# Opening of a spectral mixing and SoLU kernel: rows passed between partitions on chip instead of through DRAM, and one queue for the loads

## The chip, the cores and the metric

The kernel runs on one core of one Trainium2 chip. A core has five engines that run side by side: TensorE (matrix products; PE in the profile), VectorE (DVE), ScalarE (ACT), GpSimd (POOL) and SyncE (SP), and 16 DMA engines that carry out the transfers the others issue. The metric is the time of one execution on the device in microseconds; lower is better.

## The reference

The input x has 8 batch elements of 3136 rows and 256 channels. Each channel is filtered by a Fourier transform along the rows, a product with a complex filter, and the transform back. The result, 25088 tokens of 256, goes through a feed-forward block: a product with w_in to 1024, SoLU (h times its softmax), a layer norm with gain g, and a product with w_out back to 256.

```python
def _attn_ref(x, filt_r, filt_i):
    X = np.fft.rfft(x, axis=1)
    F = (filt_r + 1j * filt_i)[None, :, :]
    return np.fft.irfft(X * F, n=x.shape[1], axis=1).astype(np.float32)

def _moe_ref(x, w_in, w_out, g_ln):
    h = x @ w_in
    e = np.exp(h - np.max(h, axis=-1, keepdims=True))
    sm = e / (np.sum(e, axis=-1, keepdims=True) + 1e-09)
    solu = h * sm
    mu = np.mean(solu, axis=-1, keepdims=True)
    var = np.mean((solu - mu) ** 2, axis=-1, keepdims=True)
    ln = (solu - mu) / np.sqrt(var + 1e-06) * g_ln
    return (ln @ w_out).astype(np.float32)
```

The weights w_in and w_out are 64-bit floats in memory; the kernel makes 32-bit floats of them with integer operations.

## The kernel before

The transform of 3136 = 49 × 64 rows is done in two steps. The first step (`pa`) is a product along the 49, with results for 25 residues s in four parts a, and 32 columns n. They lie with (s, a) along 100 partitions and n along the row. The second step works in seven *units* of up to four residues, and wants (a, n), 128 of them, along the partitions. So the rows have to change partitions twice: from the first step to the units (`t2`), and from the units (`g`) to the step back (`t4`, `py`). For all batch elements but the first this lies beside the main loop. For the first, element 0, it is the *opening*: nothing of the main loop can start before it.

In the kernel before, rows change partitions by way of DRAM: `store_first` writes them to `d1`, `fetch` reads them as units; `store` writes to `d2`, `fetch_back` reads. Unit 0 alone is passed on chip, by 16 small transfers.

```python
    d1 = [dram.tile([NS, P, C], FP32, name=f"d1_{e}") for e in range(B)]
    d2 = [dram.tile([NS, P, C], FP32, name=f"d2_{e}") for e in range(B)]
# ... (helpers of the class Spectrum)
        def first(self, i, halves, ps, evac, out=None):

            n0, n = 2 * halves[0], 2 * len(halves)
            if out is None:
                out = self.pools["t1"].tile([NK, n, C], FP32, name=f"t1_{self.e}_{i}_{n0}", tag="t1")
            self.t1s[i, n0] = t1 = out
            for j, u in enumerate(halves):
                nc.tensor.matmul(out=ps[0:NK, j], lhsT=wf_t, rhs=self.xs[i][0:NR, 2 * u:2 * u + 2, :],
                                 start=True, stop=True)
            evac(out=t1.rearrange("p n c -> p (n c)"), in_=ps[0:NK].rearrange("p a b -> p (a b)"))


        def store_first(self, i, n0, store):
            t1 = self.t1s.pop((i, n0))
            store(d1[self.e].rearrange("s (a n) c -> (s a) n c", a=4)[
                :, NCH * i + n0:NCH * i + n0 + t1.shape[1], :], t1)
# ...

        def fetch(self, i, dma, out=None):
            self.t2s[i] = self.buffer(i, "t2", [P, 4, C]) if out is None else out
            rows, n = self.rows(i, d1[self.e])
            dma(out=self.t2s[i][:, 0:n, :], in_=rows)
# ...
        def multiply(self, i, part, add):

            residues, w = self.shape(i)
            rows = slice(0, NQ * residues)
            f = self.fs[i][rows, 0:w]

            out, term = (self.buffer(i, kind, [P, 2, C])[rows, 0:w, :]
                         for kind in (("pr", "pi")[part], "pt"))
            re, im = (ps[rows, 0:w, :] for ps in self.spectra[i])
            nc.vector.tensor_tensor(out=out, in0=re, in1=f[:, :, part, :], op=ALU.mult)
            nc.vector.tensor_tensor(out=term, in0=im, in1=f[:, :, 1 - part, :], op=ALU.mult)
            add(out=out, in0=out, in1=term, op=(ALU.subtract, ALU.add)[part])
            self.prods.setdefault(i, []).append(out)
            if part == 1:
                del self.fs[i], self.spectra[i]

        def inverse(self, i, pss):
            de, prods = self.des.pop(i), self.prods.pop(i)
            for r in range(2):
                for u in range(self.shape(i)[0]):
                    rows = slice(NQ * u, NQ * u + NQ)
                    self.product(i, pss[u][NQ * r:NQ * r + NQ], lambda v: de[rows, v, 1, r, :],
                                 prods[r][rows])
            self.gs[i] = self.buffer(i, "g", [P, 4, C])
            for u in range(self.shape(i)[0]):
                w = self.shape(i)[1]
                nc.scalar.copy(out=self.gs[i][:, u:2 * w:2, :], in_=pss[u][:, 0:w, :])

        def store(self, i, dma):
            rows, n = self.rows(i, d2[self.e])
            dma(out=rows, in_=self.gs.pop(i)[:, 0:n, :])
```

What `convert` ends with, after its VectorE operations:

```python
            if share:
                nc.scalar.mul(rest, lo, 2.0 ** -44)
                nc.gpsimd.tensor_tensor(out=rest, in0=rest, in1=power.bitcast(FP32), op=ALU.mult)
            else:
                stt(out=rest, in0=lo, scalar=2.0 ** -44, in1=power.bitcast(FP32), op0=ALU.mult,
                    op1=ALU.mult)
            nc.gpsimd.tensor_tensor(out=dst, in0=dst, in1=rest, op=ALU.add)
```

The opening in program order:

```python
        st.enter_context(tc.manual_schedule())
        nc.sync.dma_start(out=wf_t, in_=wf_dram)
        pieces = NH // NCH

        fetch_x(0, 0, NCH, 0, N1 - 1, nc.sync.dma_start)
        fetch_x(0, 0, NH, N1 - 1, 1, nc.sync.dma_start)
        for i in range(pieces):
            if i:
                fetch_x(0, NCH * i, NCH, 0, N1 - 1, nc.sync.dma_start)
            fetch_x(1, NCH * i, NCH, 0, N1, nc.gpsimd.dma_start)
            if i in (4, 7):
                begin(i // 7)
        load_tables(0, 4, nc.gpsimd.dma_start)
        load_tables(4, 4, nc.gpsimd.dma_start)
        for i in range(pieces):
            sp.xs[i] = rows_x[:, NCH * i:NCH * i + NCH]

            sp.first(i, (0, 1), ps_h.tile([P, 2, 512], FP32, name=f"pa_0_{i}", tag="h"),
                     nc.scalar.copy, sp.xs[i][0:NK])
            sp.store_first(i, 0, lambda out, in_: by_16((nc.scalar.dma_start, nc.sync.dma_start), out, in_))

        def idle(out):

            nc.tensor.matmul(out=out, lhsT=tables[0][0][:, 0, 0].rearrange("p u q -> p (u q)"),
                             rhs=filters[0][0][:, 0], start=True, stop=True)

        def idle_row(count, name):
            for j in range(count):
                idle(ps_h.tile([P, 2, C], FP32, name=f"{name}_{j}", tag="h"))

        idle_row(8, "idle")

        def convert(j):
            load_float64(weights[j][0], raws.pop(j), negate=j < 4, share=j < 4)

        for j in range(2):
            convert(j)

# ...
        def start(i):
            sp.fetch_filter(i)
            sp.fetch_de(i)
            sp.forward(i, halves(f"pb_0_{i}"))

        units = len(sp.units)

        sp.t2s[0] = t2_0 = pools["t2"].tile([P, 4, C], FP32, name="t2_0_0", tag="t2")
        for n in range(16):
            (nc.sync, nc.scalar)[n % 2].dma_start(
                out=t2_0[NH * (n % 4):NH * (n % 4) + NH, n // 4, :], in_=rows_x[n:n + 1])
        for i in range(1, units):
            sp.fetch(i, nc.sync.dma_start, spare_piece(i - 1))
            if i == 2:
                load_tables(8, NP - 8, nc.sync.dma_start)
        for i in range(2):
            start(i)
        for i in range(units):
            if i + 2 < units:
                start(i + 2)
            sp.multiply(i, 0, nc.vector.tensor_tensor)
            sp.multiply(i, 1, nc.gpsimd.tensor_tensor)
            pss = [ps_t.tile([P, 2, C], FP32, name=f"pc_0_{i}_{u}", tag="t") for u in range(2)]
            idle(pss[0])
            sp.inverse(i, pss)
            sp.store(i, nc.scalar.dma_start)
            if i == 0:
                nc.gpsimd.dma_start(out=wi_t, in_=wi_dram)
                nc.gpsimd.dma_start(out=wq_t, in_=wq_dram)
                nc.gpsimd.dma_start(out=g_sb, in_=moe_g_ln.rearrange("(k p) -> p k", p=P))
            elif i != 2:
                begin({1: 2, 3: 3, 4: 4, 5: 5, 6: 6}[i])
        idle_row(14, "idler")
        rows_t4 = pools["r"].tile([P, NH, C], FP32, name="t4_0", tag="r")
        for ch in range(pieces):
            t4s[0, ch] = rows_t4[0:NK, NCH * ch:NCH * ch + NCH]
        for ch in range(pieces):
            fetch_back(0, ch, None, by_16)
        fetch_second()
        for i0, n, rows in ((0, 4, P), (4, 4, P), (8, NP - 9, P), (NP - 1, 1, NQ)):
            f, at = filters[i0]
            nc.sync.dma_start(
                out=f_dram[i0:i0 + n].rearrange("i u q k c -> (u q) i (k c)")[0:rows],
                in_=f[0:rows, at:at + n].rearrange("p i k c -> p i (k c)"))
        convert(2)
        begin(7)
        convert(3)
        convert(4)
        weight_sums(w_in_sb)
        for j in (5, 6, 7):
            convert(j)
        for ch in range(pieces):
            for cb in range(KD):
                back(0, ch, cb, nc.scalar.copy)
```

`fetch_x` loads rows of x, half h = 0 forward and h = 1 backward. `begin(j)` loads a piece of weights as 64-bit words (512 KB), `convert(j)` takes it apart: eight to ten VectorE operations, one or two GpSimd operations and, with `share`, a ScalarE scaling. `load_tables` loads the transform tables `de` and the filters `f`. `idle` is a product whose result nobody uses; it keeps TensorE at work while it would wait. The order of instructions on each engine is that of the program.

## Time and profile before

| | |
|---|---|
| time, median of 3 runs | 1681.72 us (1679.47 to 1682.98) |
| span of the profiled execution | 1680.2 us |
| TensorE busy | 1597.7 us (95%) |
| VectorE, ScalarE, GpSimd busy | 75%, 56%, 67% |
| moved by DMA | 311.72 MB, mean 186 GB/s |
| first product of the first step | at 9.34 us |
| first product of a unit (pb) | at 45.28 us |
| first product of the step back (py) | at 90.93 us |
| first product of the main loop (m) | at 107.50 us |

The profile names an instruction by its engine, its line in the kernel and its tiles, as `py<-wi_t,t` for what is written and read. Behind each group stands how long its engine sat idle before it, and what ended that. The chain of waits goes back from the last instruction to what released it, and so on; the stretches on it set the time, whatever other engines are doing.

### The profile page before, as it was taken

To read this page: it belongs to the slowest core of one execution; us is meant where nothing else is said; L and a number is where in the kernel's file an instruction comes from. 1 tells how busy PE (TensorE), PEld (TensorE's weight loads), DVE (VectorE), ACT (ScalarE), POOL (GpSimd) and SP (SyncE) were. 2 spreads that over 40 slices of the span, in tenths; PEclk is the share of its full clock that TensorE was granted. 3 is DMA by queue.
4 is the path that set the end of the run, shared out by engine and by line. 5 is a ranking of instruction groups with operands and counts; after the bars stand their busy time and mean duration, and the time that the engine had idled before them with its cause. 6 is when DMAs were issued, how large, how long until landed. Compare 5 with 4: busy or idle time off the path is not lost.

```text
span 1680.2 us, 31072 instructions
## 1 busy us (share of the span) xinstructions
PE 1597.7 (95%) x10022; PEld 1094.7 (65%) x10022; DVE 1260.4 (75%) x2619; ACT 939.3 (56%) x1730; POOL 1120.8 (67%) x1268
## 2 busy tenths in 40 slices
PE   5798899999999999999999999999999999999996
PEld 1353356766766676667766676667776777777776
DVE  1676887788777877886878777887778767787773
ACT  2154455656655565566655656556565566655551
POOL 4444786577676766697577866687576766676674
PEclk8999999999999999999999999999999999999999
DMA  9886868786787668865786667766775444444443
GB/s 264 254 278 202 255 180 243 196 220 182 191 224 222 178 182 236 228 182 150 210 243 195 176 166 220 229 181 161 204 213 161 117 125 123 103 106 105 109 112 95
DMA packets 375957, 311.72 MB, mean 186 GB/s; under 512 B 61514, under 2 KB 341571, under 8 KB 375795
## 3 DMA queue, kind: packets, MB, share of 16 engines
q1 hardware_dynamic: 306260, 169.81, 38.5%
q0 software_dynamic: 32640, 101.65, 20.5%
q10 hardware_dynamic: 36896, 38.28, 8.2%
q8 instruction: 81, 1.33, 0.3%
q14 instruction: 80, 0.66, 0.1%
HBM read 124.83 MB, written 81.50 MB: 123 GB/s over the span
## 4 chain that ended last, share of the span: by engine, by line
PE 64%; DMA 17%; DVE 8%; POOL 3%; issue 3%; SPq 2%; ACT 1%; ACTq 0%; DVEq 0%; POOLq 0%
PE m L680 26%; PE o L792 25%; DMA solu_t<-turn 7%; PE py L353 5%; DMA x<-in_x_dram 2%; DMA t<-d 2%; PE pa L260 2%; PE pb L292 2%; PE pc L292 2%; SPq L750 2%; DVE h L728 2%; DVE turn L738 1%; DMA out_dram<-ot 1%; PE pa L217 1%; DVE diff L245 1%
## 5 line engine op out<-in xcount | busy, mean ns | idle before, releaser
L730 ACT ACTIVATE e<-h,nmu 128x1024 f32<-128x1024 f32 x196 | 225.3, 1149 | 360.3 <-DVE h L728 358.8
L792 PEld LDWEIGHTS o<-w_out_sb,solu_t 128*128 128x128 f32 x3136 | 380.3, 192 | 57.8 <-issue 40.7
L792 PE MATMUL o<-w_out_sb,solu_t 128*128 128x128 f32 x3136 | 400.5, 276 | 9.1 <-DVE rsum L723 6.3
L680 PE MATMUL m<-w_in_sb,s 128*128 128x512 f32 x784 | 401.8, 604 | 4.6 <-ACT h L690 2.5
L792 PEld LDWEIGHTS o<-w_out_sb,u 128*128 128x128 f32 x2352 | 305.2, 191 | 147.4 <-issue 113.8
L658 POOL TENSOR_TENSOR u<-solu_t 128x512 f32<-128x512 f32 x98 | 145.3, 1483 | 311.0 <-DMA solu_t<-turn 179.0
L680 PE MATMUL m<-w_in_sb,y 128*128 128x512 f32 x588 | 313.8, 617 | 15.9 <-DVE nmax L704 12.8
L792 PE MATMUL o<-w_out_sb,u 128*128 128x128 f32 x2352 | 312.3, 276 | 7.0 <-ACT ot L804 6.3
L728 DVE SCALAR_TENSOR_TENSOR h<-e,rsum,h 128x1024 f32<-128x1024 f32 x196 | 289.1, 1475 | 6.9
L811 DVE SCALAR_TENSOR_TENSOR ot<-o,rs_t,ot 128x128 f32<-128x128 f32 x294 | 102.5, 349 | 206.6 <-ACT ot L804 170.3
L690 ACT COPY h<-m 128x512 f32<-128x512 f32 x294 | 173.5, 590 | 130.8 <-PE m L680 116.2
L738 DVE STREAM_TRANSPOSE turn<-h 128x1024 f32<-128x1024 f32 x196 | 242.3, 1236 | 0.8
L712 ACT ACTIVATE e<-h,nmax 128x1024 f32<-128x1024 f32 x196 | 226.1, 1154 | 0.0
L658 POOL TENSOR_TENSOR u<-solu_t,u 128x512 f32<-128x512 f32 x98 | 142.7, 1456 | 87.2 <-PE o L792 83.3
L704 DVE CUSTOM_DVE_ANT_0 h<-m,h 128x512 f32<-128x512 f32 x196 | 133.2, 679 | 82.2 <-ACT h L690 59.3
L680 PEld LDWEIGHTS m<-w_in_sb,y 128*128 128x128 f32 x588 | 95.1, 192 | 124.5 <-DVE nmax L704 67.9
L356 ACT COPY y<-py 128x392 f32<-128x392 f32 x128 | 109.6, 856 | 105.4 <-PE py L353 103.8
L353 PEld LDWEIGHTS py<-wi_t,t 100*128 100x128 f32 x1024 | 132.3, 192 | 53.9 <-issue 40.4
L680 PEld LDWEIGHTS m<-w_in_sb,s 128*128 128x128 f32 x784 | 124.0, 191 | 65.9 <-issue 45.7
L658 POOL TENSOR_TENSOR solu_t<-solu_t,solu_t 128x512 f32<-128x512 f32 x98 | 150.8, 1538 | 7.7
L658 POOL TENSOR_TENSOR u<-u,solu_t 128x512 f32<-128x512 f32 x98 | 136.9, 1397 | 0.7
L353 PE MATMUL py<-wi_t,t 100*128 100x98 f32 x1024 | 131.6, 273 | 0.7 <-DMA t<-d 0.4
(108 smaller groups left out, 1978.3 us busy)
## 6 DMA issues: line engine op xcount, KB each, us to landing
solu_t<-turn SPq DMA_DIRECT2D x784, 128.0 KB
out_dram<-ot SPq DMA_DIRECT2D x196, 128.0 KB
t<-d POOLq DMA_DIRECT2D x56, 400.0 KB, 4.9
d<-x POOLq DMA_DIRECT2D x100, 200.0 KB, 5.3
f<-f_dram POOLq DMA_DIRECT2D x39, 512.0 KB, 6.9
d<-g POOLq DMA_DIRECT2D x39, 512.0 KB, 5.1
t<-d ACTq DMA_DIRECT2D x36, 512.0 KB
x<-in_x_dram SPq DMA_DIRECT2D x112, 98.0 KB
```

The costliest lines, as they stand in the source:

```text
L353: nc.tensor.matmul(out=psv[:, i:2 * NCH - i:2 * NCH - 1 - 2 * i, :], lhsT=t4s[e, ch][:, i, cb * P:cb * P + P], rhs=wi_t, start=True, stop= ...
L356: evac(out=y[:, cb, t0:t0 + S].rearrange("p (r m j) -> p m j r", m=N2 // NCH, j=NCH)[:, ch:last + 1 - ch:last - 2 * ch], in_=psv.rearrange ...
L658: nc.gpsimd.tensor_tensor(out=out, in0=in0, in1=in1, op=op)
L680: nc.tensor.matmul(out=ms[j, bank], lhsT=lhsT, rhs=w_in_sb[:, w, :], start=m in (1, 2, 7), stop=True, skip_group_check=True)
L690: nc.scalar.copy(out=h_half(k, i), in_=ms[j, 0])
L704: nc.vector.tensor_tensor_reduce(out=h_half(k, i), in0=ms[j, bank], in1=h_half(*kept), scale=1.0, scalar=sofar, op0=ALU.add, op1=ALU.min, ...
L712: nc.scalar.activation(out=e, in_=hs[k], func=AFT.Exp, bias=nmaxs.pop(k)[:, 1:2], scale=-1.0, accum_out=esum)
L728: nc.vector.scalar_tensor_tensor(out=solu, in0=e, scalar=rsum, in1=solu, op0=ALU.mult, op1=ALU.mult, accum_out=nmu)
L730: nc.scalar.activation(out=e, in_=solu, func=AFT.Square, bias=nmu, scale=-float(DFF), accum_out=variances[g][:, i:i + 1])
L738: nc.vector.transpose(out=turns[g][:, :, i, :], in_=solus.pop(k).rearrange("p (f j) -> p f j", j=32))
L792: nc.tensor.matmul(out=pos[p, bank], lhsT=lhs[:, f, :], rhs=w[:, f, :], start=f == 0 and m in (1, 2, 7), stop=True, skip_group_check=True)
L811: nc.vector.scalar_tensor_tensor(out=ot, in0=pos[p, bank], scalar=rs, in1=out_half(p, *kept)[0], op0=ALU.mult, op1=ALU.add)
```

## The change

The change keeps the rows on chip. After the first step, 25 transfers, one for each residue, move 4 partitions × 32 rows of 256 to 128 partitions × one row; seven units use them. After the units, 25 transfers do the opposite. All are issued by GpSimd. The stores to `d1` and `d2` of element 0 and the fetches from them go away. All loads from DRAM in the opening move to SyncE's queue, in the order in which they are needed; the 49 rows of a half are loaded as 48 and 1, and as 45 and 4. Loads of weights come earlier, three of the eight conversions rather than two stand ahead of the units, and the rows of useless products are shortened from 8 to 6 and from 14 to 7. It is for a shorter wait between the first step, the units and the step back.

```diff
--- before.py
+++ after.py
@@ -163,15 +163,6 @@
                     yield (slice(NQ * u + 32 * quarter, NQ * u + 32 * quarter + 32), k, held,
                            filter_rows(filt, quarter, u, i0, held))
 
-    def whole(dmas, out, in_):
-        dmas[0](out=out, in_=in_)
-
-    def by_16(dmas, out, in_):
-
-        n = 45 if out.shape[0] == N1 else out.shape[0] // 16 * 16
-        dmas[0](out=out[:n], in_=in_[:n])
-        dmas[1](out=out[n:], in_=in_[n:])
-
     class Spectrum:
 
 
@@ -335,14 +326,12 @@
 
     t4s = {}
 
-    def fetch_back(e, ch, rows_pool, split=None):
-
-        split = split or whole
-        if rows_pool is not None:
-            t4s[e, ch] = rows_pool.tile([P, NCH, C], FP32, name=f"t4_{e}_{ch}", tag="r")[0:NK]
-        split(
-            (nc.sync.dma_start if split is by_16 else nc.gpsimd.dma_start, nc.sync.dma_start), t4s[e, ch],
-            d2[e].rearrange("s (a n) c -> (s a) n c", a=4)[:, NCH * ch:NCH * ch + NCH, :])
+    def fetch_back(e, ch):
+
+        t4s[e, ch] = pools["r"].tile([P, NCH, C], FP32, name=f"t4_{e}_{ch}", tag="r")[0:NK]
+        nc.gpsimd.dma_start(
+            out=t4s[e, ch],
+            in_=d2[e].rearrange("s (a n) c -> (s a) n c", a=4)[:, NCH * ch:NCH * ch + NCH, :])
 
     def back(e, ch, cb, evac):
 
@@ -366,7 +355,7 @@
 
         def load_words(src, n):
             raw = wpool.tile([P, 512, 2], I32, name=f"raw_{n}", tag="raw")
-            nc.gpsimd.dma_start(
+            nc.sync.dma_start(
                 out=raw.rearrange("p (k d) w -> p k d w", d=src.shape[-2]) if len(src.shape) == 4 else raw,
                 in_=src)
             return raw
@@ -470,22 +459,29 @@
         nc.sync.dma_start(out=wf_t, in_=wf_dram)
         pieces = NH // NCH
 
-        fetch_x(0, 0, NCH, 0, N1 - 1, nc.sync.dma_start)
-        fetch_x(0, 0, NH, N1 - 1, 1, nc.sync.dma_start)
+
         for i in range(pieces):
-            if i:
-                fetch_x(0, NCH * i, NCH, 0, N1 - 1, nc.sync.dma_start)
-            fetch_x(1, NCH * i, NCH, 0, N1, nc.gpsimd.dma_start)
-            if i in (4, 7):
-                begin(i // 7)
-        load_tables(0, 4, nc.gpsimd.dma_start)
-        load_tables(4, 4, nc.gpsimd.dma_start)
+            for h in range(2):
+                rows = (N1 - 1, N1 - 4)[h]
+                fetch_x(h, NCH * i, NCH, 0, rows, nc.sync.dma_start)
+                if i == 0:
+                    fetch_x(h, 0, NH, rows, N1 - rows, nc.sync.dma_start)
+            if i == 4:
+                begin(0)
+        begin(1)
+        for j, (i0, n) in enumerate(((0, 4), (4, 4), (8, NP - 8))):
+            load_tables(i0, n, nc.sync.dma_start)
+            if j < 2:
+                begin(j + 2)
+        nc.sync.dma_start(out=wi_t, in_=wi_dram)
+        nc.sync.dma_start(out=wq_t, in_=wq_dram)
+        nc.sync.dma_start(out=g_sb, in_=moe_g_ln.rearrange("(k p) -> p k", p=P))
+        begin(4)
         for i in range(pieces):
             sp.xs[i] = rows_x[:, NCH * i:NCH * i + NCH]
 
             sp.first(i, (0, 1), ps_h.tile([P, 2, 512], FP32, name=f"pa_0_{i}", tag="h"),
                      nc.scalar.copy, sp.xs[i][0:NK])
-            sp.store_first(i, 0, lambda out, in_: by_16((nc.scalar.dma_start, nc.sync.dma_start), out, in_))
 
         def idle(out):
 
@@ -496,13 +492,10 @@
             for j in range(count):
                 idle(ps_h.tile([P, 2, C], FP32, name=f"{name}_{j}", tag="h"))
 
-        idle_row(8, "idle")
+        idle_row(6, "idle")
 
         def convert(j):
-            load_float64(weights[j][0], raws.pop(j), negate=j < 4, share=j < 4)
-
-        for j in range(2):
-            convert(j)
+            load_float64(weights[j][0], raws.pop(j), negate=j < 4, share=j < 3)
 
         def start(i):
             sp.fetch_filter(i)
@@ -511,14 +504,32 @@
 
         units = len(sp.units)
 
-        sp.t2s[0] = t2_0 = pools["t2"].tile([P, 4, C], FP32, name="t2_0_0", tag="t2")
-        for n in range(16):
-            (nc.sync, nc.scalar)[n % 2].dma_start(
-                out=t2_0[NH * (n % 4):NH * (n % 4) + NH, n // 4, :], in_=rows_x[n:n + 1])
+
+        sp.t2s[0] = pools["t2"].tile([P, 4, C], FP32, name="t2_0_0", tag="t2")
         for i in range(1, units):
-            sp.fetch(i, nc.sync.dma_start, spare_piece(i - 1))
-            if i == 2:
-                load_tables(8, NP - 8, nc.sync.dma_start)
+            sp.t2s[i] = spare_piece(i - 1)
+
+        def residues(i):
+            for s in range(4 * i, min(4 * i + 4, NS)):
+                yield slice(4 * s, 4 * s + 4), s - 4 * i
+
+        convert(0)
+        for i in range(units):
+            for rows, s in residues(i):
+                nc.gpsimd.dma_start(out=sp.t2s[i][:, s, :], in_=rows_x[rows])
+            if i in (1, 3):
+                convert((i + 1) // 2)
+        for j in (5, 6, 7):
+            begin(j)
+        rows_t4 = pools["r"].tile([P, NH, C], FP32, name="t4_0", tag="r")
+        for ch in range(pieces):
+            t4s[0, ch] = rows_t4[0:NK, NCH * ch:NCH * ch + NCH]
+
+        def store(i):
+            g = sp.gs.pop(i)
+            for rows, s in residues(i):
+                nc.gpsimd.dma_start(out=rows_t4[rows], in_=g[:, s, :])
+
         for i in range(2):
             start(i)
         for i in range(units):
@@ -526,34 +537,22 @@
                 start(i + 2)
             sp.multiply(i, 0, nc.vector.tensor_tensor)
             sp.multiply(i, 1, nc.gpsimd.tensor_tensor)
+            if i:
+                store(i - 1)
             pss = [ps_t.tile([P, 2, C], FP32, name=f"pc_0_{i}_{u}", tag="t") for u in range(2)]
             idle(pss[0])
             sp.inverse(i, pss)
-            sp.store(i, nc.scalar.dma_start)
-            if i == 0:
-                nc.gpsimd.dma_start(out=wi_t, in_=wi_dram)
-                nc.gpsimd.dma_start(out=wq_t, in_=wq_dram)
-                nc.gpsimd.dma_start(out=g_sb, in_=moe_g_ln.rearrange("(k p) -> p k", p=P))
-            elif i != 2:
-                begin({1: 2, 3: 3, 4: 4, 5: 5, 6: 6}[i])
-        idle_row(14, "idler")
-        rows_t4 = pools["r"].tile([P, NH, C], FP32, name="t4_0", tag="r")
-        for ch in range(pieces):
-            t4s[0, ch] = rows_t4[0:NK, NCH * ch:NCH * ch + NCH]
-        for ch in range(pieces):
-            fetch_back(0, ch, None, by_16)
+        store(units - 1)
+        idle_row(7, "idler")
         fetch_second()
         for i0, n, rows in ((0, 4, P), (4, 4, P), (8, NP - 9, P), (NP - 1, 1, NQ)):
             f, at = filters[i0]
             nc.sync.dma_start(
                 out=f_dram[i0:i0 + n].rearrange("i u q k c -> (u q) i (k c)")[0:rows],
                 in_=f[0:rows, at:at + n].rearrange("p i k c -> p i (k c)"))
-        convert(2)
-        begin(7)
         convert(3)
-        convert(4)
         weight_sums(w_in_sb)
-        for j in (5, 6, 7):
+        for j in range(4, 8):
             convert(j)
         for ch in range(pieces):
             for cb in range(KD):
@@ -876,7 +875,7 @@
         assert S * (e - 1) <= P * (back_at[0] // 2 * 2) and P * (back_at[-1] + 2) <= S * e // P // 2 * 2 * P
         for ch, t in enumerate(back_at):
             row_loads.append((
-                t, t - 1, spectrum_at[-1] + 2, lambda e=e, ch=ch: fetch_back(e, ch, pools["r"])))
+                t, t - 1, spectrum_at[-1] + 2, lambda e=e, ch=ch: fetch_back(e, ch)))
             for cb in range(KD):
                 (early, late)[cb][t].append(
                     lambda e=e, ch=ch, cb=cb: back(e, ch, cb, nc.scalar.copy))
```

## The prediction

> **What bounds the kernel now.** I read the page first. Its first part gives TensorE 1597.7 us busy of a span of 1680.2 us, so the main loop is bound by matmuls and has nothing to give. The change touches only the opening, so the question is how long the opening is and which wait ends last in it. The second part shows where TensorE is not full:
>
> ```profile
> PE   5798899999999999999999999999999999999996
> ```
>
> Each digit is 42 us. Only the first four slices, 168 us, have room (the last is the tail, which is not changed). The largest gain that a perfect opening could bring is therefore some tens of microseconds, one or two per cent.
>
> Next I asked for the chain of waits over the first 110 us (start, length, what; the pieces of the units and those of a few hundredths are left out):
>
> ```profile
> 1.35 7.95 DMA x<-in_x_dram
> 9.34 8.51 PE pa L217 x12
> ...
> 18.92 7.71 DMA d<-x
> 26.70 6.53 DMA d<-x
> 33.25 8.10 DMA t<-x
> 41.37 4.71 DMA t<-x
> 46.09 7.40 DMA f<-in_filt_r_dram
> 53.51 5.59 DMA y<-d
> ...
> 78.88 12.21 PE idler L492 x28
> 91.09 0.88 PE py L353 x8
> ...
> 100.10 6.81 DMA y<-in_x_dram
> ...
> 108.21 5.83 DMA f_dram<-f
> ```
>
> From 18.92 to 59.10 us the chain is nothing but transfers: rows of the first step out to DRAM (d<-x), back in (t<-x, y<-d), and one table load (f) between them. The 12.21 us of "idler" are matmuls without a use; they fill the wait for the second round trip (d<-g, then t<-d). After 91 us come the first step back (py, 16.6 us long) and the main loop, whose first product starts at 107.50.
>
> Third, the windows of these stages (duration, busy time of TensorE, its weight loads, VectorE, ScalarE, GpSimd, granted clock, DMA share, GB/s):
>
> ```profile
> 28.00:48.00 20.00, 10.66 (x35) 4.06 (x39) 2.37 (x5) 1.36 (x3) 10.86 (x14) 0.74 0.93 255
> 59.00:79.00 20.00, 18.11 (x149) 8.49 (x150) 14.34 (x25) 5.37 (x10) 7.71 (x9) 0.89 0.86 282
> 79.00:91.00 12.00, 12.00 (x29) 5.30 (x29) 11.65 (x17) 1.73 (x3) 6.18 (x5) 1.00 0.82 254
> 107.50:131.00 23.50, 20.63 (x46) 7.08 (x46) 10.01 (x31) 11.37 (x19) 14.65 (x27) 1.00 0.92 320
> ```
>
> Between 28 and 48 us VectorE works 2.37 us and the DMA engines are 93% busy: this stage is bound by transfers. Between 59 and 79 us, when the data are there, the units go at about 3 us each. Lastly, what GpSimd pays to issue a transfer and for an addition, from the groups by form:
>
> ```profile
> L428 POOL DMA_DIRECT2D f<-in_filt_i_dram x8 | 4.5, 560 | 9.7 <-DMA de<-de_tbl 4.8 <-DMA raw<-in_moe_w_in_dram 2.5 <-DMA x<-in_x_dram 1.9
> L315 POOL TENSOR_TENSOR pi<-pi,pt 128x512 f32<-128x512 f32 x6 | 7.6, 1272 | 19.2 <-DVE pt L314 17.8 <-PE pb L292 1.4
> ```
>
> An issue takes 560 ns; with the gap to the next (two of them: 1.13 us) I count 0.6 us. The 9.7 us idle before them shows GpSimd held up by earlier transfers that had not landed.
>
> [...] with three issuers the DMA share is 0.93 to 0.95 up to 48 us, and still the table and the pieces that are needed first come last. [...] The trace before has the one-row load of x as a single packet of 32,768 bytes, 2.59 us long[...]; transfers with 4 rows on one side and 128 on the other it does not have. [...] the same VectorE conversion step (L383) takes 0.42 us alone and 1.53 us beside a GpSimd addition.
>
> **The change part by part.** All by the clock of the trace.
>
> *The loads.* SyncE issues nine transfers in 5.58 us, 0.62 us each. The first piece now needs four of them (48, 1, 45 and 4 rows), issued from 1.18 to 3.66 us. The small tables wi_t and wq_t landed 3.5 and 3.1 us after their issue, and the 32 KB single packet takes 2.59 us, so about 8.0 us instead of 9.34.
>
> *The first step.* From 9.34 to the end of the last copy of pa at 28.12 us are 18.8 us, of which 1.35 us are the wait of ScalarE for its own stores; these go away. 8.0 + 17.4 = 25.4 us.
>
> *What GpSimd does before the first transfer.* In program order the conversion of the first weight comes ahead: one ScalarE scaling (0.68 us) behind the copies and two GpSimd operations (1331 and 1312 ns): 25.4 + 0.7 + 2.65 = 28.8 us.
>
> *Rows to the units.* Removed: eight 384 KB and eight 16 KB stores, 16 small on-chip transfers, six fetches (five of 512 KB). In their place 25 on-chip transfers of 128 KB, all from GpSimd: 25 × 0.6 = 15 us, with two more conversions of 2.65 us between them: 28.8 + 15 + 5.3 = 49.1 us. Only then comes the first GpSimd addition (pi of unit 0), without which no unit goes back: in the program of the change all 25 stand ahead of it on GpSimd. So the first inverse starts about where the before has it (its pi was at 51.66), although its rows arrive some 12 us earlier. This is the step that costs the change most of its gain.
> The DMA side allows this narrowly. One queue carries x 3.2 MB, weights 4.2, tables 1.7 and filters 3.4, in all 12.5 MB; at 306 GB/s (what 10 to 27 us moved) that is 41 us. The 3.2 MB on chip cost, at 46 ns for a 1 KB packet (median of the uncontended packet records), 3136 × 46 / 16 = 9 us more. So both are through at about 50 us; what unit 0 and 1 need (5.9 MB) is in at about 22 us.
>
> *Units and the way back.* Per full unit GpSimd now has one addition (1.27) and four issues (2.4), 3.7 us, against 3.0 us for the unit's other work: GpSimd sets the pace. 49.1 + 6 × 1.27 + 0.77 + 25 × 0.6 = 72.5 us for the last issue, and 3 to 5 us to land, since the filters' stores to DRAM now run at the same time: about 77 us for the first py, instead of 90.93. That is 14 us. It agrees with the fill of 7 instead of 14 useless products (0.86 us a product, 6.0 instead of 12.2 us).
>
> *The rest of the opening.* py takes 16.6 us as before: the main loop starts at 93.6 instead of 107.5. In the window 107.5 to 131, 2.9 us are idle, mainly behind y<-in_x_dram and f_dram<-f; both are now issued well before the products and I count 2 us of it as gained. VectorE must have converted four w_out pieces: it can start the sums after the last conversion's GpSimd addition, at about 73.9, and has 3.7 + 4 × 4.7 = 22.5 us: 96.4 us. The main loop first needs VectorE 3.2 us after its start (110.66 against 107.50), at 96.8. So this just fits and costs nothing.
>
> Sum: 14 + 2 = 16 us. 1681.7 − 16 = 1665.7; I say 1666.
>
> **The rivals.** *GpSimd becomes the bound more sharply than I have it.* In the before each of its issues waited for landings as soon as about eight were out, with 7 to 10 us from issue to landing. If the 25 transfers share engines with the load queue packet by packet, a 1 KB packet waits for a 4 KB one (46 + 159 ns) and 32 of them take 6.6 us; four run together, so 1.6 us per transfer for as long as the queue is full. For: the DMA share of 0.93. Against: the queue should be empty by 45 to 50 us. If it holds, the first addition comes at 55 to 58 and the gain falls to 7 to 9 us: 1673.
> *The conversions of VectorE replace the wait.* If they end at 100 to 104 rather than 96, the main loop begins early but stops at its first maximum; the gain is 8 to 10 us: 1672. For: VectorE was busy without a gap from 76 to 110 us in the before. Against: three rather than two conversions are now done ahead of the units.
> *Everything fits better than my serial sum.* If issues of on-chip transfers take 0.5 us and landings overlap, the py start at 71 and all 2.9 us are saved: 1659.
> *Nothing gained since the main loop hid it.* It cannot: with TensorE 95% busy overall and full after slice four, a later or earlier start shifts all that follows.
>
> **Range and chances.** The first two rivals give 7 to 10 us, the good case 22 to 23 us. The runs of before differ by 3.5 us. So 1656 to 1675 should hold it 8 times in 10. Two per cent is 33.6 us; to reach 1648 the main loop would have to start at 74 instead of 107.5, about when the last GpSimd issue goes out by my sum, and before any py. To lose 2% the 25 transfers would have to run at a fraction of their rate. Faster by over 2%: 0.03; within 2%: 0.95; slower by over 2%: 0.02.
>
> **What would show it.** Right: no d<-x, y<-d, d<-g or t<-d of batch element 0; first pa at about 8 us; 25 GpSimd transfers from 29 to 49 us; pi of unit 0 at 49; GpSimd busy without a gap to 72; first py at 77; first m at 94; DMA share over 0.9 up to 45 us. Wrong: idle GpSimd between the transfers waiting for earlier ones (first rival); nmax waiting for VectorE (second); py more than 5 us off 77; or a main loop that is longer or shorter than before, which nothing here would explain.

## The result, and the profile after

The changed kernel takes 1744.09 us (median of 4 runs, 1740.82 to 1751.32); the kernel before, beside it, 1681.32. The ratio is 1.038, with a 95% interval of 1.0343 to 1.0416: it is slower by 3.8%, where I had predicted 1666 us and given 0.02 to a loss of over 2%.

Where the 63 us arise is seen from the first start of each stage, read from the trace (us):

| kernel | first unit's product (pb) | first inverse (pc) | first step back (py) | py lasts | first main product (m) |
|---|---|---|---|---|---|
| before | 45.28 | 51.12 | 90.93 | 16.55 | 107.50 |
| predicted | about 33 | about 49 (first addition) | 77 | 16.6 | 93.6 |
| after | 37.19 | 59.67 | 144.43 | 27.59 | 171.82 |

The main loop begins 64.3 us later than before and then takes 1568.3 us instead of 1572.7 (each is the profiled span less the first m). So the whole loss lies in the opening. Part 2 of the page after, TensorE's busy tenths and its granted clock (in tenths of full speed) in 40 slices of 43.5 us, shows it in the first four slices:

```profile
PE   6548888999999999999999999999999999999996
PEclk8665989999999999999999999999999999999999
```

Before, the same PE row began 5798: slices two and three have lost two and five tenths, and the clock there is down to 0.6. The chain of waits after, over the first 200 us (start, length, what), names the engine that TensorE waits for:

```profile
33.86 13.15 DMA y<-x
...
72.25 12.98 DMA t<-g
...
90.56 16.47 DMA t<-g
...
133.74 10.49 DMA t<-g
...
144.43 27.59 PE py L342 x128
```

Not the issues of GpSimd stand here, as in my sum, but the transfers themselves: rows to the units (y<-x), rows from the units (t<-g), each 10 to 16 us long where I had counted 3 to 5. The waits from 30 to 145 us (who, for what, us in total, times, longest) say the same:

```profile
ACT g L321 <- DMA t<-g: 60.2, 5, 21.1
```

ScalarE's copy of g waited 60.2 us in five pieces for t<-g, since a copy writes into a buffer of g that earlier transfers still read. GpSimd's timeline shows the two sides (start, busy, what, idle time before and who ended it):

```profile
29.78 3.42 POOL L519 DMA_DIRECT2D t<-x  x4
...
62.03 1.27 POOL L306 TENSOR_TENSOR pi<-pi,pt 128x512 f32<-128x512 f32 x1
...
90.56 2.07 POOL L531 DMA_DIRECT2D t<-g  x3 [10.26 <-ACT g L321]
```

The first transfer goes out at 29.78 (predicted 28.8), but the first addition comes at 62.03 instead of 49. Between them GpSimd stands still ten times for landings, from its eleventh transfer on, 9.2 us in all. On the way back it is idle too: 10.26 us behind ScalarE, which itself waits for t<-g. Windows of three stages after (start and end, length, busy time of TensorE, weight loads, VectorE, ScalarE, GpSimd, then granted clock, DMA share, GB/s):

```profile
72.00:90.00 18.00, 3.73 (x24) 2.24 (x24) 3.36 (x4) 0.33 (x1) 8.01 (x10) 0.59 1.07 173
90.00:144.00 54.00, 24.57 (x78) 8.88 (x78) 17.89 (x34) 4.34 (x9) 17.66 (x22) 0.66 0.78 133
144.00:172.00 28.00, 27.57 (x129) 27.60 (x130) 12.63 (x21) 12.60 (x15) 2.79 (x2) 0.50 0.09 31
```

From 72 to 90 us the DMA engines are busy all the time (the share passes 1 because a packet counts where it starts), yet move 173 GB/s; the windows of before, at a share of 0.82 to 0.93, moved 254 to 320. No computing engine is busy even half of the time. In the third line TensorE is busy throughout, at half clock: py takes 27.6 instead of 16.6 us.

### The profile page after: what moved, and what is told of

It is laid out like the page before. It is cut to its first block, busy times and chain, and to the rows that moved or that the text cites. A ratio compares the mean times of both kernels' runs of the same rounds, so it can differ in the third digit from the quotient of the medians.

```text
span 1740.1 us, 31008 instructions
## 1 busy us (share of the span) xinstructions
PE 1620.5 (93%) x10004; PEld 1110.5 (64%) x10004; DVE 1253.1 (72%) x2620; ACT 936.4 (54%) x1729; POOL 1133.1 (65%) x1280
## 4 chain that ended last, share of the span: by engine, by line
PE 65%; DMA 18%; DVE 7%; issue 4%; POOL 3%; SPq 2%; ACT 1%; ACTq 0%; DVEq 0%; POOLq 0%
PE m L679 26%; PE o L791 26%; PE py L342 6%; DMA solu_t<-turn 6%; DMA t<-g 3%; PE pa L251 2%; DMA y<-x 2%; DMA x<-in_x_dram 2%; PE pc L283 2%; PE pb L283 2%; SPq L749 2%; DVE turn L737 1%; DMA t<-d 1%; DVE h L727 1%; DMA de<-de_tbl 1%
## 5 line engine op out<-in xcount | busy, mean ns | idle before, releaser
L679 PE MATMUL m<-w_in_sb,y 128*128 128x512 f32 x588 | 314.7, 619 | 13.8 <-DVE nmax L703 11.3
L342 PEld LDWEIGHTS py<-wi_t,t 100*128 100x128 f32 x1024 | 144.7, 209 | 60.6 <-issue 48.0
L342 PE MATMUL py<-wi_t,t 100*128 100x98 f32 x1024 | 143.0, 290 | 8.2 <-DMA t<-g 7.5
```

What stands on the lines that cost most here:

```text
L342: nc.tensor.matmul(out=psv[:, i:2 * NCH - i:2 * NCH - 1 - 2 * i, :], lhsT=t4s[e, ch][:, i, cb * P:cb * P + P], rhs=wi_t, start=True, stop= ...
L679: nc.tensor.matmul(out=ms[j, bank], lhsT=lhsT, rhs=w_in_sb[:, w, :], start=m in (1, 2, 7), stop=True, skip_group_check=True)
```

## The experiments

Three theories for slow transfers stood against each other. *Port,* as the expectations call it: each transfer has one side of four neighbouring partitions, and their place makes it slow; with four that lie far apart it would be quick. I had not thought of it in the prediction. *Load:* the transfers are slow because they share the DMA engines with the loads from DRAM. *GpSimd:* its queue and its waits are the bound. ENGINES in the expectations is the theory that the few packets a transfer keeps under way are the limit, wherever its partitions lie.

**Transfers by themselves.** This kernel computes nothing of the reference. Stage by stage it writes two tiles and then moves rows of them, 128 KB a transfer, as in the change.

```diff
+        def near(s):
+            return slice(4 * s, 4 * s + 4)
+        def spread(s):
+            first = s % 4 * 6 + s // 4
+            return slice(first, first + 3 * NS + 1, NS)
...
+            for j, s in enumerate(residues or range(count)):
+                ends = (units[:, j, :], rows[where(s)])
+                out_, in_ = ends if there else ends[::-1]
+                (dma or nc.gpsimd.dma_start)(out=out_, in_=in_)
```

`near` takes the change's four neighbours, `spread` four partitions that lie 25 apart. Expected:

> Transfers of 128 KB between 4 partitions and 128 partitions by themselves, with nothing else on the chip; nothing of the reference is computed. Three theories. PORT: [...] Then one transfer of neighbours takes 6 to 7 us from issue to landing against 3 to 4 for one whose four rows lie 25 partitions apart; two residues 8 apart [...] take clearly longer than two that are 1 apart; four and eight neighbours 7 to 13 us, spread 4 to 7. ENGINES: [...] neighbours and spread take the same. LOADS: the on-chip transfers are only slow because they share engines with the load queue; then everything by itself is quick (eight in 7 us at most) and only the stages with loads beside them are slow, neighbours and spread alike. From SyncE's queue, four transfers should be slower than from GpSimd [...].

The timeline of this kernel shows each stage as GpSimd's issues and the next write of VectorE, which starts when the last of them has landed. The way back with eight neighbouring transfers, and further down eight spread ones:

```profile
296.66 5.45 POOL L37 DMA_DIRECT2D rows<-units  x8 [19.33 <-DVE units L29]
316.65 6.88 DVE L28 MEMSET rows<- 128x8192 f32 x1 [20.28 <-issue]
...
359.51 5.45 POOL L37 DMA_DIRECT2D rows<-units  x8 [15.37 <-DVE units L29]
372.74 6.88 DVE L28 MEMSET rows<- 128x8192 f32 x1 [13.53 <-issue]
```

So 20.0 against 13.2 us, with nothing else under way. All stages, each measured once, from first issue to that write, and in brackets the time in which data moved by the packet records, loads included (us); residues 0 and 1 are two near transfers that lie 4 partitions apart, residues 0 and 8 two that lie 32 apart:

| | there, near | there, spread | back, near | back, spread |
|---|---|---|---|---|
| 1 transfer | 8.8 (5.20) | 5.1 (1.57) | 8.5 (4.31) | 6.1 (2.50) |
| 4 | 11.1 (7.41) | 8.1 (3.88) | 12.7 (7.61) | 8.8 (5.18) |
| 8 | 18.0 (13.21) | 11.5 (7.48) | 20.0 (15.07) | 13.2 (9.38) |
| 8, and 2 MB of loads | 18.9 (15.38) | 18.5 (14.5) | 26.4 (21.66) | 17.6 (13.53) |
| residues 0 and 1 | 9.8 (6.01) | | 10.1 (5.44) | |
| residues 0 and 8 | 13.8 (10.41) | | 13.8 (8.79) | |

One near transfer there runs in packets of 4096 bytes of 618 ns, about four at a time; a spread one in packets of 159 ns, a quarter of that: 128 KB take 5.20 us, which are 25 GB/s, against 1.57. Residues 0 and 8 together need 10.41 us with packets of 1174 ns; residues 0 and 1 only 6.01. So with nothing else under way the place of the partitions sets the pace; by what means, these records don't show. A row of transfers suffers from it too: four near ones there have up to 16 packets under way at a time, but take 7.41 us, and eight take 13.21. At the pace of the eight, 25 of them would need, as an estimate, 41 us there (25/8 of 13.21) and 47 back (25/8 of 15.07), before any load stands beside them; I had counted 9 us for the way there, and for the way back only the landing of the last one. With loads beside them, spreading helps only on the way back (26.4 to 17.6 us; there 18.9 to 18.5).

**One half undone.** First the way back again through DRAM, the way there on chip as in the change:

```diff
-            for rows, s in residues(i):
-                nc.gpsimd.dma_start(out=rows_t4[rows], in_=g[:, s, :])
+            sp.gs[i] = g
+            sp.store(i, nc.scalar.dma_start)
...
         idle_row(7, "idler")
+        for ch in range(pieces):
+            fetch_back_0(ch)
```

> The change with its way back undone: units are stored to DRAM by ScalarE and fetched by SyncE as in the kernel before; the rows to the units stay on chip. If the way back is where most of the loss lies (units at 11 us each from 75 to 134 us), py starts at about 95 us and the time is 1690 to 1705. If the way there costs as much, 1710 to 1720.

Then the way there through DRAM, the way back on chip:

```diff
+            sp.store_first(i, 0, split)
...
-            for rows, s in residues(i):
-                nc.gpsimd.dma_start(out=sp.t2s[i][:, s, :], in_=rows_x[rows])
+            if i == 0:
...
+            else:
+                sp.fetch(i, nc.sync.dma_start, sp.t2s[i])
```

> The change with its way to the units undone: stores of the first step to DRAM and fetches as before; the way back stays on chip. If the way back is most of the loss, the units start at 45 to 50 us but still take 10 to 11 us each, py at 125 to 135 us, time 1725 to 1735. If the way there is the larger part, 1700 or less.

Measured: 1685.83 us for the first (2 runs; ratio to before 1.0003, 0.997 to 1.0036), less than I had expected, and 1740.84 for the second (2 runs; 1.0329, 1.0296 to 1.0362), more than I had expected. The way back is what costs. In the chain of waits of the first, the last unit's rows go out (d<-g) and come in (t<-d) in one round trip:

```profile
90.36 2.65 DMA d<-g
...
93.75 4.33 DMA t<-d
...
98.22 1.12 PE py L349 x8
```

In the second, py starts at 145.58, hardly later than after (144.43), although its first inverse came at 73.12 and not at 59.67. So the transfers back set their own pace, whatever comes before them. Nor does the way there gain anything by itself: with it alone the first piece of py starts at 95.71 and the second, which the chain shows, at 98.22; before it was 90.93.

**Place or load.** The rows of the first step can be spread by permuting the columns of the first table, at the price of two small tables more:

```diff
+    row_of = np.array([NS * a + (s if s == NS - 1 else s % 4 * 6 + s // 4) for s in range(NS) for a in range(4)])
...
+    wf0_t = consts.tile([NR, NK], FP32, name="wf0_t")
+    wi0_t = consts.tile([NK, NR], FP32, name="wi0_t")
...
-                yield slice(4 * s, 4 * s + 4), s - 4 * i
+                first = s if s == NS - 1 else s % 4 * 6 + s // 4
+                yield slice(first, first + 3 * NS + 1, NS), s - 4 * i
```

> The change, but the first step puts the four parts of a residue 25 partitions apart instead of next to each other (columns of the first table and rows of the last one permuted for element 0)[...]. Everything else as in the change, two small tables more. PORT: on-chip transfers land in 4 to 6 us instead of 10.7 and 15.8, the first py comes at 80 to 95 us instead of 144, and the time is 1670 to 1690. ENGINES or LOADS: little changes, 1735 to 1750.

Measured: 1751.17 us (4 runs; 1.0394, 1.0359 to 1.043). py starts at 127.20, 17 us earlier but not at 80 to 95, and a transfer back lands after 11.2 us (median), not after 4 to 6. Its packets of 4096 bytes have a median of 186 ns instead of 459 (packet records of GpSimd's queue, 72 us to the start of py). The total is not better: from the first m on this kernel takes some 24 us more. In that stretch the transfers of 512-byte packets (SyncE's queue, mainly solu_t<-turn, 800 to 1500 us) have a mean of 36.0 ns, against 31.6 in the kernels before and after. The two new tables take 392 and 400 bytes of each partition and move all that lies behind them by 792. To test this, the same kernel with tables padded to 512 bytes each, so that the rest moves by 1024:

```diff
+    wf0_t = consts.tile([NR, P], FP32, name="wf0_t")[:, 0:NK]
+    wi0_t = consts.tile([NK, P], FP32, name="wi0_t")[:, 0:NR]
```

> The spread rows again, with the two extra tables padded so that they take 1024 bytes of a partition instead of 792. In the first spread run py came 17 us earlier than in the change, but the main loop took 24 us longer and its 512-byte packets 36 instead of 31.6 ns. If the shifted place in SBUF is the cause of that, the packets are back at 32 ns and the time is 1720 to 1728 (main loop from 155, 1568 to 1573 us long). If it was the two tables in DRAM or the chip, it is 1745 to 1752 again.

Measured: 1717.44 us (2 runs; 1.0185, 1.0136 to 1.0234), packets back at 31.6 ns, py at 114.87. Nothing but the place of the buffers differs, so this was the cause of the longer main loop. Why py too comes 12 us earlier than without padding is open.

The load theory, with the change's neighbouring rows: all loads and stores that don't concern the opening (three pieces of w_out, rows of the next element, the filters' stores) go behind the units, on GpSimd's queue.

```diff
-        for j in (5, 6, 7):
-            begin(j)
...
         store(units - 1)
         idle_row(7, "idler")
+        for j in (5, 6, 7):
+            begin(j, nc.gpsimd.dma_start)
```

> The change with the load queue silenced while units go back: the last three w_out pieces, the second element's rows and the filters' stores to DRAM are issued by GpSimd behind its last on-chip transfer, instead of by SyncE from 71 us on. The on-chip transfers are those of the change. To be read by the first py, not by the total (GpSimd's conversions now wait behind 19 more issues). By the stages measured alone, four transfers of neighbours move in 7.4 us and eight in 15, so if the load queue is what stretches them to 16 to 22 us here, a unit takes 7 instead of 11 us and py starts at 112 to 122 us. [...]

And both edits together, with the padded tables:

```diff
-                yield slice(4 * s, 4 * s + 4), s - 4 * i
+                first = s if s == NS - 1 else s % 4 * 6 + s // 4
+                yield slice(first, first + 3 * NS + 1, NS), s - 4 * i
...
+            begin(j, nc.gpsimd.dma_start)
```

> Both: spread rows (padded) and the silenced load queue. Alone, eight spread transfers took 7.5 us back to back on the DMA engines there and 9.4 back, about what GpSimd needs to issue them (5.4). If port and load queue together explain the slow way back, units go at 4 to 5 us each and py starts at 100 to 108 us. If something else holds it, above 115.

Each ran once: 1740.96 and 1706.25 us, beside 1684.83 for before. What they were made for is the time up to py, the median from issue to landing of the 25 transfers back (the view of DMA issues over the first 200 us; after and both are shown), and ScalarE's waits for them (from 30 us to py):

```profile
t<-g POOLq DMA_DIRECT2D x25, 128.0 KB, 15.8
...
t<-g POOLq DMA_DIRECT2D x25, 128.0 KB, 5.4
```

| | t<-g lands after | ScalarE waits for t<-g | first py | py lasts |
|---|---|---|---|---|
| after | 15.8 us | 60.2 us | 144.43 | 27.59 |
| quiet queue | 10.1 | 38.4 | 124.53 | 27.60 |
| spread (padded) | 9.7 | 26.4 | 114.87 | 27.60 |
| both | 5.4 | 18.1 | 100.52 | 16.41 |

On the way back the place of the partitions and the load each have their part (30 us of the time to py, of which only 17 came without padding, and 20; 44 together), and none is the story alone. Each row is one profiled execution, so a difference of one or two us is not to be read: in two kernels that are the same up to there, the first addition comes at 62.03 and 60.83. The quiet queue's py lies just outside the 112 to 122 that I had given for the load theory; with both, py lies in the range given. With both lessened a landing takes 5.4 us, close to the 3 to 5 that I had predicted. *GpSimd* can't be the main bound, since with both edits it still issues all 50 transfers and py comes 44 us earlier. But it has a part in what is left: py still comes 9.6 us later than before, and the first addition at 60.64, behind all 25 issues, where a later kernel with the additions on VectorE has it at 47.59.

The way there is another matter. Neither edit shortens it much: the landings of y<-x take 10.7 us in after, 11.3 with the quiet queue and 9.8 with spread rows, and the first addition comes at 62.03, 63.07 and 58.78. Its loads, which the units need, stay in all these kernels. From 29 to 62 us the packets of the rows take 56% of the 16 engines' time and those of the loads 43%, together all of it. That the loads are what delays the rows there is not tested.

The totals don't follow py here. Both kernels with a quiet queue load the last weights later, so that VectorE converts them later, and TensorE stands in the main loop. A window of the kernel with both:

```profile
127.00:146.90 19.90, 3.54 (x9) 1.15 (x8) 18.04 (x41) 2.93 (x5) 12.69 (x18) 0.71 0.30 88
```

TensorE works 3.5 of 19.9 us there, VectorE 18.0: the rival that I had called the conversions of VectorE, brought about by my own edit.

**The clock of the step back.** The change, with eight useless products behind each unit from the third on, and eighteen rather than seven at the end:

```diff
             sp.inverse(i, pss)
+            if i >= 2:
+                idle_row(8, f"idle_u{i}")
         store(units - 1)
-        idle_row(7, "idler")
+        idle_row(18, "idler")
```

> The changed kernel with eight useless products behind each unit from the third on, and eighteen instead of seven at the end, so that TensorE has no long pause before the step back. If the low clock of the step back comes from TensorE's pauses while it waits for the slow transfers: the step back starts at 144 to 146 as before but takes 16.6 to 19 instead of 27.6 us, the main loop starts at 161 to 165, the time is 1732 to 1737. Rival, the clock has another cause: the step back stays at 27.6 us and the time at 1742 to 1746.

Measured: 1736.39 us (4 runs; 1.0307, 1.0275 to 1.0338). The window in which py begins:

```profile
144.00:162.00 18.00, 17.82 (x105) 13.17 (x104) 17.48 (x31) 8.60 (x10) 4.21 (x3) 1.00 0.15 53
```

The clock is 1.00 instead of 0.50, py starts at 150.67 (the useless products end only then) and lasts 16.5 us; the main loop begins at 167.18 instead of 171.82. The low clock of py after (0.50), where TensorE had stood idle for 7.5 us just before, was thus a consequence of its waiting, and 11 us of the loss.

**The part of the change that is worth keeping.** Way there on chip with spread rows (one more table, padded to 1024 bytes), additions of the units on VectorE, so that none waits behind 25 transfers, way back through DRAM:

```diff
-            sp.multiply(i, 1, nc.gpsimd.tensor_tensor)
+            sp.multiply(i, 1, nc.vector.tensor_tensor)
```

> A version meant to beat both: rows to the units on chip, [...] the way back through DRAM as in the kernel before, and the units' additions on VectorE (0.69 us each), so that no unit waits for GpSimd to get through its 25 issues. With the way back in DRAM alone (additions on GpSimd) py started at 98 and the time was that of the kernel before. Now units should follow their rows, the last at about 70 us, py at 80 to 86 us, and the time be 1666 to 1674. If the rows themselves come too late (they need until 66 us beside the loads), 1678 to 1685.

Measured: 1678.56 us (4 runs, 1674.75 to 1686.92; 0.9947, 0.9908 to 0.9985), in the range that I had given for rows that come too late. py starts at 87.02, 3.9 us earlier than before but just outside 80 to 86. And TensorE's timeline of the profiled run, the slowest of the four, has a pause ahead of py:

```profile
79.43 6.28 PE L502 MATMUL idler<-f,de 128*128 128x512 f32 x14
87.02 3.23 PE L355 MATMUL py<-wi_t,t 100*128 100x98 f32 x20 [1.31 <-DMA t<-d]
```

After 1.31 us of idleness py ran at a mean clock of 0.54 and lasted 26.3 us. Hence two more, with nine and with twelve useless products instead of seven:

```diff
-        idle_row(7, "idler")
+        idle_row(9, "idler")
```

> The run before (rows there on chip [...], additions on VectorE, rows back through DRAM) had its step back at 87.0 us, 26.3 us long at a granted clock of 0.54, after a pause of TensorE of 1.3 us; here nine instead of seven useless products stand ahead of it, which close that pause. If the pause lowers the clock: the step back again starts at 87 to 88, takes 16.6 us, the main loop starts at 104 to 106, and the time is 1667 to 1673. Rival, the clock is lowered by something else (the load of the units before, or chance): the step back keeps its 26 us, the main loop starts at 113 and the time stays at 1677 to 1682.

```diff
-        idle_row(9, "idler")
+        idle_row(12, "idler")
```

> The same kernel with twelve useless products instead of nine ahead of the step back: with nine, the rows of the last unit took 8.7 us to DRAM instead of 4.7, so TensorE still paused 2.2 us and the step back ran at a clock of 0.53 again. Twelve end at about 89.4 us, after the last landing of either run (87.0 and 88.9). If a pause of one to two microseconds costs the clock: no idle time ahead of the step back, which starts at 89 to 90, takes 16.4 to 17 us, the main loop starts at 106 to 107, and the time is 0.988 to 0.994 of before. Rival, the load since 60 us lowers the clock whatever precedes: 26 us again, the main loop at 115, and 0.995 to 0.998.

With nine, the round trip of the last unit was longer in the profiled run, TensorE still paused 2.17 us, and py again took 26 us at 0.53; 1679.78 us (6 runs; 0.9961, 0.9932 to 0.9991). It didn't test what it was made for. With twelve there is no pause, as TensorE's timeline shows:

```profile
90.17 16.53 PE L355 MATMUL py<-wi_t,t 100*128 100x98 f32 x128
106.80 2.02 PE L694 MATMUL m<-w_in_sb,y 128*128 128x512 f32 x4
```

1677.10 us (6 runs, 1673.88 to 1679.29; 0.9948, 0.993 to 0.9967). The stages are where I expected them, the ratio just above the 0.988 to 0.994 that I had given. This beats the kernel before by half a per cent, and the changed one by about four. Of the half per cent, how much is due to the spread rows and how much to the additions on VectorE was not separated; near rows with the additions on GpSimd gave nothing (1.0003). Twelve products instead of seven don't show in the median (0.9948 and 0.9947); the six runs lie 5.4 us apart instead of 12 to 17.

## Why the prediction was wrong

*The loads and the first step* held to within 1.3 us: first pa at 9.33 (8.0 predicted, so the shorter way to the first piece gave nothing), GpSimd's first transfer at 29.78 (28.8).

*Rows to the units* is the first step that failed, in its term "25 × 0.6 = 15 us": 32.3 us passed from the first transfer to the first addition instead of 20.3. An issue takes 0.68 us, near enough to 0.6; the rest are 9.2 us in which GpSimd waited for landings. I had let the transfers run beside the issues, at 46 ns for a 1 KB packet and spread evenly over 16 engines: 9 us for all of the way there. That size came from the packets of other transfers. These run in packets of 4096 bytes, with medians of 276 ns there (29 to 62 us) and 459 back. Four transfers do keep up to 16 packets under way, but that is not enough: by itself, with four neighbours on one side, a transfer has packets of 618 ns, where one with its partitions far apart has packets of 159. On the way there, though, spreading didn't help much; that the loads are the reason there stays open.

*One queue of loads, empty at 50 us* failed with it: by the packet records SyncE's queue still moved 2.3 MB from 40 to 70 us. Loads and rows hold each other up: by themselves, the same 2 MB of loads moved in 16.3 us beside eight near transfers back and in 10.5 beside spread ones, and in the kernel with the quiet queue the transfers back land after 10.1 us instead of 15.8.

*Units and the way back*, "GpSimd sets the pace" and "3 to 5 us to land", is the step that cost most: 82.4 us from the first addition to py instead of 28, which is 54 of the 78 us between the predicted and the measured start of the main loop. A landing took 15.8 us; the buffers of g came free that late, ScalarE waited 60.2 us for them, and from the fourth on each unit took 11 to 14 us instead of 3.7. Only GpSimd's issues were in my sum for this way; that the transfers themselves need more than the issues was not. The way back through DRAM alone takes the whole loss away.

*"py takes 16.6 us as before"* was right in its work and wrong in its clock: 27.6 us at 0.50, as TensorE had waited. These are the last 11 us; they go when TensorE is kept at work, as the run with added useless products shows (16.5 us at 1.00). 13 + 54 + 11 = 78.

*The first rival* had named what happened, transfers that share engines and GpSimd that waits for landings, but sized it with 1.6 us for a transfer and only as long as the load queue is full. *The conversions of VectorE* came into it only in the experiments. That *"the 25 transfers would have to run at a fraction of their rate"*, my ground for 0.02 on slower, was the right condition. The profile before has no transfer between four partitions and 128, and I took that for a missing detail instead of a cost that nothing had measured. It did hold a sign, in the chain that I had shown: unit 0's 512 KB on chip, in 16 transfers with a single partition on one side, stand in it with 8.10 and 4.71 us (t<-x), where 512 KB fetched from DRAM take 5.59 (y<-d). I passed over it. My range held rivals of 7 to 10 us, all built on the one packet time.

## What to carry to other kernels

Count a transfer by its narrow side: how many partitions it has there, how far apart they lie, and what a transfer of that shape was measured to take, not by bytes over 16 engines. Passing rows between partitions on chip saves a round trip, but four neighbouring partitions moved 128 KB in 5.20 us and four far apart in 1.57, and beside 2 MB of loads that gain all but went away on the way there (18.9 and 18.5 us for eight). Spreading can be had by permuting a constant table; the table takes room, and where it moved the other buffers by 792 bytes that cost more than the spreading had gained (some 24 us of the main loop, for a py 17 us earlier). Where a prediction rests on a kind of transfer that the profile doesn't contain, its rate is the largest unknown, and the range has to hold it.

## What the runs showed of the hardware that I had not expected

- Two transfers of the same shape need 6.01 us if their four partitions lie 4 apart, and 10.41 if they lie 32 apart.
- From SyncE, four near transfers there took 19.1 us (15.5 of data) where GpSimd's took 11.1 (7.41), in packets of 1024 bytes instead of 4096 and with three packets under way in the mean, six at most, where GpSimd's had 12 and 16. Why, the records don't show.
- Moving the buffers of a kernel by 792 bytes of each partition made 512-byte packets from one place on chip to another slower (36.0 instead of 31.6 ns) and the main loop some 20 us longer; moving them by 1024 did not (31.6 ns). What it is in 792 bytes that matters, no run tells.
- At half clock the step back did not bring the clock back up: in the changed kernel it ran for 27.6 us without a pause at 0.50, after 7.5 us of idleness (mean clock 1.00 from 134 to 137, 0.72 in the idle 137 to 144). Once the main loop's products ran, 1.00 was back within about 4 us (0.72 from 172 to 176, 1.00 from 176 to 182). With seven and nine useless products it began at full clock, after pauses of 1.31 and 2.17 us, and fell to half some 2 and 1 us later, to stay there as long as py lasted (with nine: 1.00 from 86 to 89, a mean of 0.53 from 89 to 105). The windows with seven show it (py from 87.02 on):

```profile
86.00:92.00 6.00, 4.92 (x30) 4.78 (x30) 5.86 (x11) 2.56 (x3) 1.40 (x1) 0.75 0.97 261
92.00:98.00 6.00, 6.00 (x30) 6.00 (x30) 5.79 (x11) 2.59 (x4) 1.41 (x1) 0.50 0.88 219
```

  Yet with both edits (spread and quiet) a pause of 1.2 us left it at full clock (py lasts 16.41 us), and so did, with the way back through DRAM, pauses of 0.32 and 0.51 us (1.00 from 95 to 113). What makes the clock fall after 1.31 us and not after 1.2, and why 27.6 us of py brought no rise where some 4 us with the main loop's products did, these runs don't tell.
